# New step orders, an earlier load of q for pair 1, and five row groups stored by column halves in a fused sparse-attention and soft-MoE kernel

## The chip, the core and the metric

The kernel runs on one core of a Trainium2 chip. The core has five engines with a queue of instructions each: PE (TensorE: matmuls and, beside them, weight loads, called PEld), DVE (VectorE), ACT (ScalarE), POOL (GpSimd) and SP (SyncE, which here only issues DMAs). They share nothing but memory and semaphores: an instruction waits at the head of its queue until what it needs is done, and everything behind it on that engine waits too. Sixteen DMA engines move data between HBM and the core's memory SBUF; PE writes its results to a second memory, PSUM, which DVE and ACT empty. The metric is the time of one execution on the device in microseconds (us), lower is better. Times of before and after are medians of several executions.

## What is computed

Two stages, the second on the output of the first. Batch 4, 8 heads, 768 positions, head size 64; the MoE has 8 experts of 4 slots, model size 512, hidden size 1024.

```python
def _attn_ref(q, k, v):                       # q, k, v: 4 x 8 x 768 x 64, float32
    ...
    k_min, k_max = k_chunks.min(3), k_chunks.max(3)          # chunks of 32 keys
    ub = sum over d of maximum(q * k_min, q * k_max)         # per query and chunk
    ub = where(causal, ub, -1e9); top_chunks = the 6 chunks with the largest ub
    scores = where(chosen chunk and pos_q >= pos_k, scale * q @ k.T, -1e9)
    return softmax(scores) @ v

def _moe_ref(x, phi, w1, w2):                 # x: 3072 x 512
    logits = x @ phi                                         # 3072 x 32 slots
    d = softmax(logits, axis=0); slot_input = d.T @ x
    slot_out[e] = maximum(slot_input[e] @ w1[e], 0) @ w2[e]  # 8 experts, 4 slots each
    c = softmax(logits, axis=1)
    return c @ slot_out                                      # 3072 x 512
```

## The kernel before

**Tiles and stages.** The 32 (batch, head) pairs are worked on two heads at a time, as 16 pairs 0 to 15, four to a batch. For a pair, k and q are turned (`trk`, `trq`: transposes on PE, then copies on ACT, `evk`, `evq`), the chunks' minima and maxima are taken on DVE (`kmin`, `kmax`, `bd`, which DVE or, as `bdp`, POOL does), q is split into negative and positive parts (`qsn`, `qsp`), the bound is formed on PE (`ub`), the sixth largest is found and compared on DVE (`sel`, with a cast on POOL), the comparison is turned (`ns`, `evns`). Scores are made in six groups of blocks (`sc:0` to `sc:5`, a pair of matmuls for q.k and a pair that adds the mask, lines 334 and 344), ACT takes the exponential (`ex`, line 358), POOL masks the diagonal blocks (`mk`, line 368), PE multiplies by v (`pv`, line 382), DVE divides by the row sum (`norm`, lines 394 and 395), and the result is turned (`xt`, `evx`). The MoE's logits, its running maximum over batches and the sum into slots are done once per batch (`moe_...`).

**Order of the work.** Nothing is scheduled by the compiler: `tc.manual_schedule()` keeps each engine's instructions in the order in which the program emits them. A fixed list `HEAD` does pair 0 and prepares the next ones. Then step i = 1 to 15 runs down a string of words (lines 728 to 733), in which a word acts on a pair some steps away: `sc`, `ex`, `mk` on pair i, `pv` on i - 1, `norm`, `xt`, `evx` on i - 2, `ub`, `sel`, `ns`, `evns` on i + 1, `trk` to `qsp`, `bd`, `lv` on i + 2. The word `moe_x@n` acts only where i - n is a batch's last pair. Steps 1 to 4 take PLAIN, and then by i mod 4: 0 PLAIN, 1 LOGITS, 2 SLOTS, 3 AFTER; step 14 takes BEFORE_LAST and step 15 FINAL, whose words of its own are `pl:n` (parts of the last pv), `nl`, `xl`, `el`/`ela` (its norm, transposes, and their copies on DVE or ACT), `norm1`, `xt1`, `evx1` (those of pair 14), `lgt`, `lgl` (the last logits), `cs` (column sums of the combine weights, line 817), `pma` (the last maximum), `mz` (a memset on POOL) and `lh:n` (a load of weights).

**Loads.** All loads but two come from POOL's queue and turn float32 into bf16 on the way: `lv` v of a pair (192 KB, line 174), `lkq` k and q of two pairs (384 KB each, line 168, in odd steps), `lw` weights of an expert (1 MB, line 150, in steps 2, 4, 6, 8, 9, 10, 12, 13). The second weights of the last two experts come in eight pieces of 256 KB (`w_half`, line 160): pieces 0 and 1 in step 14, 2 and 3 in step 15, 4 to 7 after it. Pieces 0 to 3 are output columns 256 to 511, pieces 4 to 7 columns 0 to 255. At the start SP loads k and q of pair 0, and POOL k of pair 1 (line 168), then the identity `ident` (line 186), q of pair 1, and k and q of pairs 2 and 3.

**The end.** After step 15 the slots go through the experts: `experts_in` (line 928), then the output projection by column halves y = 1 and y = 0: `experts_out` (line 969), `shared_out` (line 995), and `last_expert_out` (line 1005), which reads the pieces of `w_half`. The 3072 output rows are stored as 12 groups of 256 rows (512 KB). The first BYHALF groups are made and stored by column halves, so that their first halves go out between the two halves of the projection; the others follow whole:

```python
    for m in range(BYHALF):
        out_half(m, 1, TAGS[m % 2])              # 2 matmuls, line 1040; store of 256 KB, line 1042
    for f in range(2):
        experts_out(0, f)
    for f in range(2):
        shared_out(0, f)
    last_expert_out(0)
    nc.vector.tensor_scalar_mul(so_sb[0], outs[0], zinv)
    for m in range(BYHALF):
        out_half(m, 0, TAGS[(m + BYHALF) % 2])
    for m in range(BYHALF, NM):                  # whole groups: line 1070, store of 512 KB, line 1076
        ...                                      # the last one as two stores, line 1074
        if m == BYHALF:
            last_rows()                          # combine weights of the last batch
```

A group's two halves of the rows are copied from PSUM by DVE (line 1029) and ACT (line 1026) side by side; SP issues the stores.

Of the kernel before, what the change touches and what calls it, by code (L numbers as in the profile page):

```python
# [59 lines left out]
def kernel(  # L60
# [13 lines left out]
    NPB = H // 2  # L74
# [88 lines left out]
    def load(i, nm, n=1):  # L163

        b, j = divmod(i, NPB)
        t = ring[nm][i // 2 % 3][:, 2 * (i % 2):2 * (i % 2 + n)]
        src = {"k": k, "q": q}[nm][b, 2 * j:2 * (j + n)]
        nc.gpsimd.dma_start(out=t, in_=src.rearrange("h (p g) d -> p h (g d)", p=P))
        for x in range(n):
            st[nm, i + x] = t[:, 2 * x:2 * x + 2]  # L170
# [15 lines left out]
    nc.gpsimd.affine_select(
        out=ident, in_=ident, compare_op=ALU.not_equal, fill=1.0, base=0,
        pattern=[[-1, P]], channel_multiplier=1,
# [9 lines left out]
    nc.vector.memset(pm_pad, 0.0)  # L198
    nc.vector.memset(pm_lo, 0.0)

    load(1, "q")
    load(2, "k", 2)
    load(2, "q", 2)
    def spread_mask(t0, t1, copy):
# [520 lines left out]
            }[name]  # L725
            moe(fn, i - off)

    PLAIN = """sc:0 trk lv sc:1 norm ex:0 ex:1 ub sc:2 pv:0 mk:0 evk pv:5 sel sc:5 mk:1 lw trq xt ex:2 pv:2 ex:5 evq pv:3:1 sc:3 kmin sc:4 kmax ex:3 ex:4 evx qsn ns mk:5 pv:4 mk:4 evns mk:2 mk:3 qsp lkq bd"""
    LOGITS = """sc:0 trk sc:2 ex:0 ub norm ex:2 sc:3 evk mk:0 lv pv:0 pv:5 pv:1 mk:2 sc:1 sel ex:3 xt kmin pv:2 trq pv:3 ex:1 evq sc:5 lw ex:5 mk:1 sc:4 evx ns kmax bd mk:3 moe_logits@2 evns mk:5 qsn lkq ex:4 moe_copy@2 moe_lo@2 mk:4 qsp pv:4"""
    SLOTS = """sc:1 ex:1 mk:1 moe_max@3 sc:2 ex:2 mk:2 ub moe_bound@3 norm sel moe_comb@3 trk evk sc:0 sc:3 ex:0 moe_exp@3 lkq ex:3 mk:3 pv:0:1:2:3 trq xt kmin evq moe_exp2@3 evx kmax bd moe_scale@3 lv lw sc:5 ex:5 mk:5 sc:4 ex:4 mk:4 ns evns mk:0 moe_dispatch@3 pv:5 moe_comb2@3 qsn qsp pv:4"""  # L730
    AFTER = """sc:0 lv trk sc:2 ex:0 ex:2 evk ub sc:1 norm pv:0 pv:5 sel ex:1 pv:2 pv:3 mk:0 sc:3 pv:1 mk:2 xt trq lw ex:3 sc:5 kmin evx evq ex:5 sc:4 ns mk:1 kmax bdp pv:4 mk:5 evns ex:4 mk:4 lkq qsp moe_ct@4 mk:3 qsn"""
    BEFORE_LAST = """lv norm sc:2 ex:2 moe_max@3 sc:4 ex:4 sc:0 moe_bound@3 moe_comb@3 mk:4 lw ub sel sc:3 pv:0 trk evk pv:2 moe_exp@3 pv:3:4:5:1 mk:2 ex:0 trq evq kmin sc:5 ex:3 mk:0 moe_comb2@3 kmax moe_exp2@3 xt ns sc:1 moe_scale@3 mk:3 lkq qsn ex:5 lh:0 evx mk:5 ex:1 qsp lh:1 evns moe_dispatch@3 moe_ct3@3 bd mk:1"""
    FINAL = """sc:1 sc:0 norm sc:2 ex:1 pv:0 pv:2 pv:3 pv:4 mk:1 ctc pv:5 pv:1 ex:0 ex:2 sc:3 xt mk:0 ex:3 norm1 sc:4 mk:2 ex:4 xt1 mk:3 evx pl:0 evx1 sc:5 mk:4 pl:2 pl:1 nl:0 pl:3 nl:1 xl:0 pl:4 el:0 mz lh:2 ex:5 pl:5 lh:3 lgt:0 xl:1 lgt:1 nl:2 lgl:0 xl:2 ela:1 lgl:1 el:2 lgl:2 pma cs"""

    BL = B - 1
    parts = {}
# [285 lines left out]
    def rows(m):  # L1022
        return out[m * 2 * P:(m + 1) * 2 * P, :].rearrange("(p x) d -> p x d", x=2)
# [40 lines left out]
    n = 0  # L1064
    for m in range(BYHALF, NM):
        o_sb = op.tile([P, 2, Dm], F32, name="o_sb", tag="o_sb")
# [8 lines left out]
        if m < NM - 1:  # L1075
            nc.sync.dma_start(out=rows(m), in_=o_sb)
        if m == BYHALF:
            last_rows()
# [30 lines left out]
```

## Time and profile before

| What | us |
|---|---|
| Median of 3 executions | 156.44 (156.4 to 156.86) |
| The profiled execution's own time | 156.91 |
| Its span, first to last instruction | 155.2 |
| PE busy | 137.7 |
| DVE busy | 122.4 |
| ACT busy | 122.0 |
| POOL busy | 95.6 |
| First store issued | 134.63 |
| Last store issued | 150.38 |

The profile is of one execution; its span lies inside its own time. Times in it count from the span's start. "Busy" is time in which an engine's instructions ran; a long chain of short waits can hide behind a high share. "Idle before" says how long an engine did nothing before an instruction and, behind an arrow, what ended that. The DMA share counts packets in flight over 16 engines, so it can be above 1. A DMA's "us to landing" runs from its issue to the last of its data.

### The profile page before, as it was taken

Reading aid. Unit: us, or ns where it says so; the run is one execution under the profiler, and the core shown is the slowest. Engines: PE = TensorE matmul, PEld = TensorE weight load, DVE = VectorE, ACT = ScalarE, POOL = GpSimd, SP = SyncE. Lnnn points to the kernel's source line nnn. Section 1 sums busy time; section 2 is a strip of 40 time slices with the busy share of each in tenths; the row PEclk is TensorE's granted clock in tenths of the full one; section 3 lists DMA queues with packets and bytes.
Section 4 is the critical chain, followed back from the end, with each engine's and each line's share of the span. In section 5 each row is a group of like instructions: output and inputs, shape, how many; then the busy total and the mean of one; then the engine's idle time right before and its main releaser. Section 6 shows DMA issues by size and latency. Waiting matters only on the chain.

```text
span 155.2 us, 6083 instructions
## 1 busy us (share of the span) xinstructions
PE 137.7 (89%) x2512; PEld 91.0 (59%) x2513; DVE 122.4 (79%) x450; ACT 122.0 (79%) x166; POOL 95.6 (62%) x196
## 2 busy tenths in 40 slices
PE   7989998999999989999999999999989999776700
PEld 2444565667667676766767675766767755553200
DVE  4777987999899999999999999999766642449800
ACT  3678999999999999999999999999886233527700
POOL 6966698964978669486936947496783980000000
PEclk9999999999999999999999999999999999999965
DMA  4999999999999999999999999999999999999995
GB/s 161 184 181 207 202 191 195 214 180 196 209 215 194 196 207 189 197 205 215 202 191 200 202 211 195 206 186 213 212 200 215 211 196 198 168 313 320 378 406 229
DMA packets 46171, 33.31 MB, mean 215 GB/s; under 512 B 26304, under 2 KB 41664, under 8 KB 46144
## 3 DMA queue, kind: packets, MB, share of 16 engines
q0 software_dynamic: 41328, 25.86, 115.0%
q1 hardware_dynamic: 4816, 7.08, 12.5%
q8 instruction: 19, 0.31, 0.7%
q14 instruction: 8, 0.07, 0.1%
HBM read 52.49 MB, written 6.29 MB: 379 GB/s over the span
## 4 chain that ended last, share of the span: by engine, by line
PE 43%; DVE 17%; ACT 11%; POOL 9%; DMA 9%; issue 4%; DVEq 0%; SPq 0%; ACTq 0%; POOLq 0%
PE at_ps L382 10%; PE sc_ps L334 10%; ACT e_sb L358 9%; PE sc_ps L344 7%; DMA w_half<-in_moe_w_dram 7%; PE tr_ps L225 5%; PE xT_ps L404 3%; PE ub_ps L284 2%; POOL w_half L160 2%; DMA w_sb<-in_q_dram 2%; DVE mx L305 2%; POOL e_sb L368 2%; PE ns_ps L316 2%; DVE o_sb L1029 2%; DVE mm L244 2%
## 5 line engine op out<-in xcount | busy, mean ns | idle before, releaser
L358 ACT ACTIVATE e_sb<-sc_ps 128x768 bf16<-128x768 f32 (+2 forms) x96 | 83.2, 928 | 4.7 <-PE sc_ps L344 4.3
L368 POOL TENSOR_SCALAR_AFFINE_SELECT e_sb<-e_sb 128x256 bf16<-128x256 bf16 x96 | 37.8, 413 | 17.9 <-ACT e_sb L358 17.6
L334 PE MATMUL sc_ps<-qT,kT 64*128 64x384 bf16 (+3 forms) x260 | 37.6, 306 | 0.9 <-ACT e_sb L358 0.7
L344 PE MATMUL sc_ps<-nsT,smask 64*128 64x384 bf16 (+2 forms) x296 | 37.6, 284 | 0.1
L382 PE MATMUL at_ps<-v_t,e_sb 128*128 128x65 bf16 x630 | 26.2, 193 | 0.2
L382 PEld LDWEIGHTS <-e_sb 128*128 128x128 bf16 x630 | 22.4, 97 | 5.2 <-issue 3.1
L305 DVE MAX8 mx<-ub_ps 128x8 f32<-128x8 f32 (+1 forms) x192 | 16.9, 165 | 4.7 <-PE ub_ps L294 4.0
L334 PEld LDWEIGHTS <-kT 64*128 64x128 bf16 x260 | 12.8, 93 | 8.0 <-issue 2.2
L174 POOL DMA_DIRECT2D v_t<-in_v_dram x16 | 16.7, 1045 | 1.0 <-DMA w_sb<-in_moe_w_dram 0.9
L344 PEld LDWEIGHTS <-smask 64*128 64x128 bf16 x296 | 14.9, 95 | 3.3 <-issue 0.4
L395 DVE TENSOR_TENSOR x_sb<-at_ps,inv 128x768 bf16<-128x768 f32 (+3 forms) x18 | 15.6, 869 | 0.6
L244 DVE TENSOR_REDUCE mm<-kT 128x24 bf16<-128x768 bf16 x16 | 15.1, 943 | 0.1
L250 DVE TENSOR_REDUCE mm<-kT 128x24 bf16<-128x768 bf16 x16 | 15.1, 943 | 0.0
L235 ACT COPY qT<-tr_ps 128x768 bf16<-128x768 bf16 x16 | 13.1, 816 | 1.7 <-PE tr_ps L225 1.7
L235 ACT COPY kT<-tr_ps 128x768 bf16<-128x768 bf16 (+1 forms) x16 | 12.7, 795 | 0.6 <-PE tr_ps L225 0.6
L415 DVE COPY xT_sb<-xT_ps 128x768 bf16<-128x768 bf16 (+2 forms) x17 | 8.8, 518 | 1.6 <-PE xT_ps L404 1.6
L150 POOL DMA_DIRECT2D w_sb<-in_moe_w_dram x14 | 10.1, 721 | 0.0
L215 PE MATMUL warm_ps<-ones_sq 128*128 128x512 bf16 x27 | 8.8, 449 | 1.1 <-DVE ones_sq L180 1.1
L284 PEld LDWEIGHTS <-qpn 128*128 128x128 bf16 x192 | 6.1, 96 | 5.1 <-issue 3.7
L404 PE MATMUL xT_ps<-ident,x_sb 128*128 128x128 bf16 x96 | 8.4, 220 | 0.2 <-DVE xT_sb L415 0.2
L284 PE MATMUL ub_ps<-bd,qpn 128*128 128x48 bf16 x192 | 7.8, 184 | 0.5 <-DVE bd L256 0.4
L308 DVE TENSOR_TENSOR ns_t<-ub_ps,mx 128x288 bf16<-128x288 f32 x16 | 7.3, 457 | 0.5
(171 smaller groups left out, 220.9 us busy)
## 6 DMA issues: line engine op xcount, KB each, us to landing
w_sb<-in_moe_w_dram POOLq DMA_DIRECT2D x14, 1024.0 KB, 17.6
out_dram<-o_sb SPq DMA_DIRECT2D x14, 256.0 KB, 3.8
v_t<-in_v_dram POOLq DMA_DIRECT2D x16, 192.0 KB, 13.9
out_dram<-o_sb SPq DMA_DIRECT2D x5, 512.0 KB, 4.4
w_half<-in_moe_w_dram POOLq DMA_DIRECT2D x8, 256.0 KB, 10.4
k_in<-in_k_dram POOLq DMA_DIRECT2D x5, 384.0 KB, 13.7
q_in<-in_q_dram POOLq DMA_DIRECT2D x5, 384.0 KB, 12.3
w_sb<-in_k_dram POOLq DMA_DIRECT2D x2, 384.0 KB, 11.7
```

The lines of the kernel that those rows point to most:

```text
L174: nc.gpsimd.dma_start(out=v_t[i % NV][:, :, :, :D], in_=v[b, 2 * j:2 * j + 2].rearrange("h (g p) d -> p h g d", p=P),)
L235: copy(t.rearrange("d (p g) -> d p g", g=NQT)[:, :, g0:g1], ps.rearrange("d g p -> d p g"),)
L244: nc.vector.tensor_reduce(mm[:, 0, 0, :], kT, axis=AX.X, op=ALU.min)
L250: nc.vector.tensor_reduce(mm[:, 1, 0, :], kT, axis=AX.X, op=ALU.max)
L284: nc.tensor.matmul(o, lhsT=qpn[:, x, t * P:(t + 1) * P], rhs=bd[:, x], start=(t == 0 and x == 0), stop=False,)
L305: nc.vector.max(mx[:, a, :], ub[:, a, :max(8, 4 * t + 4)])
L334: nc.tensor.matmul(ps[:, h, c:c + w], lhsT=kT[r, kg * P:(kg + 1) * P], rhs=qT[r, qs], start=True, stop=False,)
L344: nc.tensor.matmul(ps[:, h, c + (f - t0) * P:c + (l - t0) * P], lhsT=smask[r, x, kg].rearrange("p a b -> p (a b)"), rhs=nsT[r, (f - x * NJ ...
L358: nc.scalar.activation(e[:, :, :w], st.pop(("scps", i, g))[:, :, :w], func=ACT.Exp, scale=scale)
L368: nc.gpsimd.affine_select(out=e[:, :, c:c + P], in_=e[:, :, c:c + P], compare_op=ALU.is_ge, fill=0.0, base=0, pattern=[[0, 2], [1, P]], ch ...
L382: nc.tensor.matmul(o, lhsT=st["e", i, g][:, h, c:c + P], rhs=v_t[i % NV][:, h, kg, :D + 1], start=(kg == 0), stop=(kg == t),)
L395: nc.vector.tensor_tensor(st["x", b][:, t0:t1, 2 * j:2 * j + 2, :].rearrange("p t h d -> p h t d"), at[:, :, :, :D], inv.broadcast_to([P, ...
```

## The change

Three things. POOL issues the load of q of pair 1 right behind that of k of pair 1, ahead of `ident`. All step strings are new, and a new one, REST, takes PLAIN's place in steps 8 and 12; REST also does the transposes of a batch's combine weights (`moe_ct@5`) that AFTER did one step before (`moe_ct@4`). And BYHALF is 5.

```diff
--- before.py
+++ after.py
@@ -183,6 +183,7 @@
     for t, src in zip(stage, (k, q)):
         nc.sync.dma_start(out=t, in_=src[0, :2].rearrange("h (p g) d -> p h (g d)", p=P))
     load(1, "k")
+    load(1, "q")
     nc.gpsimd.affine_select(
         out=ident, in_=ident, compare_op=ALU.not_equal, fill=1.0, base=0,
         pattern=[[-1, P]], channel_multiplier=1,
@@ -198,7 +199,6 @@
     nc.vector.memset(pm_pad, 0.0)
     nc.vector.memset(pm_lo, 0.0)
 
-    load(1, "q")
     load(2, "k", 2)
     load(2, "q", 2)
     def spread_mask(t0, t1, copy):
@@ -725,12 +725,13 @@
             }[name]
             moe(fn, i - off)
 
-    PLAIN = """sc:0 trk lv sc:1 norm ex:0 ex:1 ub sc:2 pv:0 mk:0 evk pv:5 sel sc:5 mk:1 lw trq xt ex:2 pv:2 ex:5 evq pv:3:1 sc:3 kmin sc:4 kmax ex:3 ex:4 evx qsn ns mk:5 pv:4 mk:4 evns mk:2 mk:3 qsp lkq bd"""
-    LOGITS = """sc:0 trk sc:2 ex:0 ub norm ex:2 sc:3 evk mk:0 lv pv:0 pv:5 pv:1 mk:2 sc:1 sel ex:3 xt kmin pv:2 trq pv:3 ex:1 evq sc:5 lw ex:5 mk:1 sc:4 evx ns kmax bd mk:3 moe_logits@2 evns mk:5 qsn lkq ex:4 moe_copy@2 moe_lo@2 mk:4 qsp pv:4"""
-    SLOTS = """sc:1 ex:1 mk:1 moe_max@3 sc:2 ex:2 mk:2 ub moe_bound@3 norm sel moe_comb@3 trk evk sc:0 sc:3 ex:0 moe_exp@3 lkq ex:3 mk:3 pv:0:1:2:3 trq xt kmin evq moe_exp2@3 evx kmax bd moe_scale@3 lv lw sc:5 ex:5 mk:5 sc:4 ex:4 mk:4 ns evns mk:0 moe_dispatch@3 pv:5 moe_comb2@3 qsn qsp pv:4"""
-    AFTER = """sc:0 lv trk sc:2 ex:0 ex:2 evk ub sc:1 norm pv:0 pv:5 sel ex:1 pv:2 pv:3 mk:0 sc:3 pv:1 mk:2 xt trq lw ex:3 sc:5 kmin evx evq ex:5 sc:4 ns mk:1 kmax bdp pv:4 mk:5 evns ex:4 mk:4 lkq qsp moe_ct@4 mk:3 qsn"""
-    BEFORE_LAST = """lv norm sc:2 ex:2 moe_max@3 sc:4 ex:4 sc:0 moe_bound@3 moe_comb@3 mk:4 lw ub sel sc:3 pv:0 trk evk pv:2 moe_exp@3 pv:3:4:5:1 mk:2 ex:0 trq evq kmin sc:5 ex:3 mk:0 moe_comb2@3 kmax moe_exp2@3 xt ns sc:1 moe_scale@3 mk:3 lkq qsn ex:5 lh:0 evx mk:5 ex:1 qsp lh:1 evns moe_dispatch@3 moe_ct3@3 bd mk:1"""
-    FINAL = """sc:1 sc:0 norm sc:2 ex:1 pv:0 pv:2 pv:3 pv:4 mk:1 ctc pv:5 pv:1 ex:0 ex:2 sc:3 xt mk:0 ex:3 norm1 sc:4 mk:2 ex:4 xt1 mk:3 evx pl:0 evx1 sc:5 mk:4 pl:2 pl:1 nl:0 pl:3 nl:1 xl:0 pl:4 el:0 mz lh:2 ex:5 pl:5 lh:3 lgt:0 xl:1 lgt:1 nl:2 lgl:0 xl:2 ela:1 lgl:1 el:2 lgl:2 pma cs"""
+    PLAIN = """norm sc:0 trk ex:0 sc:1 ub pv:0 lv pv:5 sc:2 ex:1 sel mk:1 evk ex:2 sc:5 trq ex:5 mk:0 evq mk:5 pv:2 pv:3 pv:1 xt kmin sc:3 sc:4 ex:3 ex:4 kmax lw evx ns mk:4 qsn evns pv:4 mk:2 lkq mk:3 qsp bd"""
+    REST = """lv moe_ct@5 sc:1 norm trk ex:1 sc:2 ub sc:0 ex:2 pv:0:5 evk mk:2 ex:0 sc:3 trq sel mk:1 lkq xt lw pv:1 kmin pv:2 ex:3 mk:0 evx sc:5 sc:4 kmax pv:3 evq bdp mk:3 ex:5 ns qsn ex:4 evns mk:5 pv:4 mk:4 qsp"""
+    LOGITS = """sc:0 trk sc:2 ex:0 lv ub mk:0 norm lw sc:1 sel pv:0 ex:2 pv:1 pv:2:5 evk sc:3 xt ex:1 trq kmin ex:3 evx sc:5 evq sc:4 kmax mk:1 ns mk:2 ex:5 moe_logits@2 qsn mk:5 bd mk:3 evns ex:4 moe_copy@2 moe_lo@2 mk:4 qsp pv:3 pv:4 lkq"""
+    SLOTS = """sc:2 moe_max@3 ex:2 mk:2 sc:1 moe_comb@3 moe_bound@3 ex:1 ub norm sel trk evk sc:5 sc:0 ex:5 moe_exp@3 ex:0 pv:0 mk:1 pv:3 moe_exp2@3 pv:5:1 trq xt evq lkq kmin lv pv:2 kmax evx moe_scale@3 sc:4 lw ex:4 sc:3 mk:0 ns ex:3 mk:3 evns bdp moe_comb2@3 mk:4 qsn pv:4 mk:5 qsp moe_dispatch@3"""
+    AFTER = """sc:1 ex:1 norm sc:0 trk ub ex:0 sc:2 pv:0 pv:3:2 evk lv pv:5 sc:3 mk:0 sel ex:2 mk:2 kmin pv:1 xt trq ex:3 evx mk:1 kmax sc:5 sc:4 ns lkq evq lw ex:5 pv:4 bdp mk:3 qsp ex:4 evns qsn mk:4 mk:5"""
+    BEFORE_LAST = """norm sc:2 lv sc:4 moe_max@3 ex:2 ub moe_bound@3 ex:4 moe_comb@3 sel sc:0 pv:0:2 trk moe_exp@3 pv:3:4:5:1 evk mk:4 sc:3 kmin trq ex:0 moe_comb2@3 kmax evq qsp ex:3 bd moe_exp2@3 ns xt moe_scale@3 evx mk:2 mk:0 sc:1 evns ex:1 lh:0 lw sc:5 ex:5 mk:5 mk:3 qsn moe_dispatch@3 moe_ct3@3 lh:1 lkq mk:1"""
+    FINAL = """sc:1 norm sc:0 sc:2 ex:1 ex:0 pv:0:4 pv:2 pv:3:5:1 ex:2 mk:0 sc:3 ctc xt mk:1 mk:2 ex:3 mk:3 sc:4 ex:4 norm1 xt1 mk:4 sc:5 pl:0 evx evx1 ex:5 nl:0 pl:1 pl:3 lh:2 pl:2 pl:4 xl:0 nl:1 lh:3 ela:0 mz pl:5 lgt:0 lgt:1 lgl:0 nl:2 xl:2 cs xl:1 el:1 ela:2 lgl:1 lgl:2 pma"""
 
     BL = B - 1
     parts = {}
@@ -828,7 +829,7 @@
             for y in range(2):
                 w_half[LATE[i - E], y] = wt.tile([P, NFG, Dm // 2], BF16, name=f"w_half{i}_{y}")
         order = FINAL if i == LAST else BEFORE_LAST if i == LAST - 1 else PLAIN if i <= NPB else (
-            PLAIN, LOGITS, SLOTS, AFTER)[i % NPB]
+            REST, LOGITS, SLOTS, AFTER)[i % NPB]
         for what in order.split():
             if what.startswith("lh:"):
                 load_w_half(int(what[3:]))
@@ -1030,7 +1031,7 @@
 
     w_ctx.close()
     op = ctx.enter_context(tc.tile_pool(name="op", bufs=NM))
-    BYHALF = 6
+    BYHALF = 5
     o_tiles = [op.tile([P, 2, Dm], F32, name="o_sb", tag="o_sb") for _ in range(BYHALF)]
 
     def out_half(m, y, tags):
```

## The prediction

> **What bounds the kernel now.** I read the page first, then busy times by window, then the last 45 us in order of time, then each DMA from issue to landing.
>
> ```profile
> PE 137.7 (89%) x2512; PEld 91.0 (59%) x2513; DVE 122.4 (79%) x450; ACT 122.0 (79%) x166; POOL 95.6 (62%) x196
> DMA  4999999999999999999999999999999999999995
> GB/s 161 184 181 207 202 191 195 214 180 196 209 215 194 196 207 189 197 205 215 202 191 200 202 211 195 206 186 213 212 200 215 211 196 198 168 313 320 378 406 229
> ```
>
> PE is the busiest engine, but the DMA row reads 9 in 38 of 40 slices. The table by window (sum of the stretch, then PE, PEld, DVE, ACT, POOL, clock, DMA share, GB/s) says the same:
>
> ```profile
> 27.64:33.99 6.35, 6.35 (x128) 4.37 (x126) 5.98 (x25) 6.34 (x10) 5.63 (x12) 1.00 1.39 198
> 25.00:118.00 93.00, 91.24 (x1831) 64.00 (x1827) 85.92 (x320) 88.28 (x115) 68.02 (x144) 1.00 1.38 201
> 140.00:142.00 2.00, 1.70 (x11) 0.87 (x10) 1.94 (x5) 1.89 (x6) 0.00 (x0) 1.00 0.83 288
> 142.00:144.00 2.00, 1.02 (x14) 0.68 (x14) 1.43 (x4) 0.67 (x2) 0.00 (x0) 1.00 1.04 350
> 146.00:148.00 2.00, 0.32 (x2) 0.00 (x0) 1.65 (x3) 1.04 (x2) 0.00 (x0) 1.00 1.02 408
> ```
>
> Over 93 us of the steps the DMA engines' share is 1.38 (packets in flight, over 1 means always something queued). Do compute or loads end last? The chain of waits near its end, and two DMA rows (the last 1 MB of w_sb, issued at 104.65, and the last w_half, issued at 127.65; KB, us to landing):
>
> ```profile
> 127.65 10.47 DMA w_half<-in_moe_w_dram
> 138.16 0.32 PE so_last L1005 x4
> 138.50 0.50 DVE so_all L1060
> ```
> ```profile
> w_sb<-in_moe_w_dram POOLq DMA_DIRECT2D x1, 1024.0 KB, 22.7
> ```
>
> w_sb lands at 104.65 + 22.7 = 127.35 and the last of the eight 256 KB pieces of w_half at 127.65 + 10.47 = 138.12. So the eight landed one behind the other, 10.77 / 8 = 1.35 us each, and a load waits 10 to 23 us in the queue behind others. That is a stream of loads that never runs dry: it ends when its bytes are through, whenever they were issued. PE in order of time (start, duration, line, idle before it):
>
> ```profile
> 132.53 0.57 PE L1005 MATMUL so_ps<-w_half,hT_pad 128*32 128x256 bf16 x8
> 133.67 0.60 PE L1040 MATMUL oh_ps<-so_all,cT_all 128*128 128x256 bf16 x4 [0.57 <-ACT so_all L1051]
> 136.06 1.06 PE L969 MATMUL so_last<-w_sb,hT_pad 128*32 128x256 bf16 x32
> 137.59 0.28 PE L1005 MATMUL so_last<-w_half,hT_pad 128*32 128x256 bf16 x4
> 138.16 0.29 PE L1005 MATMUL so_last<-w_half,hT_pad 128*32 128x256 bf16 x4 [0.28 <-DMA w_half<-in_moe_w_dram]
> ```
>
> PE came to the last four matmuls 0.28 us before their weights. The first eight (at 132.53) are as tight: the fourth piece landed at 127.35 + 4 x 1.35 = 132.75, and the second four of that row began near 132.8. Both halves of the output projection start when weights land; compute is level with them, not behind.
>
> After that come the stores. SP's issues (start, duration) and, under each, its KB and us to landing:
>
> ```profile
> 139.97 0.53 SPq L1042 DMA_DIRECT2D out_dram<-o_sb  x1
> 143.29 0.56 SPq L1042 DMA_DIRECT2D out_dram<-o_sb  x1
> 143.96 0.58 SPq L1076 DMA_DIRECT2D out_dram<-o_sb  x1
> 147.91 1.15 SPq L1076 DMA_DIRECT2D out_dram<-o_sb  x1
> 150.38 1.15 SPq L1074 DMA_DIRECT2D out_dram<-o_sb  x1
> ```
> ```profile
> out_dram<-o_sb SPq DMA_DIRECT2D x1, 256.0 KB, 2.9
> out_dram<-o_sb SPq DMA_DIRECT2D x1, 256.0 KB, 3.0
> out_dram<-o_sb SPq DMA_DIRECT2D x1, 512.0 KB, 3.6
> out_dram<-o_sb SPq DMA_DIRECT2D x1, 512.0 KB, 4.9
> out_dram<-o_sb SPq DMA_DIRECT2D x1, 256.0 KB, 3.7
> ```
>
> The second wave of halves lands from 139.97 + 2.9 = 142.87 to 143.29 + 3.0 = 146.29: (146.29 - 142.87) / 5 = **0.68 us a half**. Whole groups land from 147.56 to 152.81 in four steps: **1.31 us each**. The last store lands at 154.08, with computing over at 147.65. Only between 140 and 142 do the engines have slack (share 0.83): the first six halves are through and the next ones have just begun.
>
> **The change part by part.**
>
> *BYHALF 6 to 5.* The sixth group leaves both waves and becomes a whole store behind them. From the start of the second wave, 5 halves and 7 whole groups have to land instead of 6 and 6: +1.31 - 0.68 = **+0.63 us**. Its half in the first wave filled the slack before the second wave, so leaving it out frees nothing. What could pay: PE comes to L1005 earlier by one group. Six groups took DVE this long:
>
> ```profile
> 133.98 2.70 DVE L1029 TENSOR_SCALAR o_sb<-oh_ps,inv_a 128x256 f32<-128x256 f32 x6 [1.99 <-DMA w_half<-in_moe_w_dram]
> ```
>
> 2.70 / 6 = 0.45 us. But PE was already 0.28 us early; it will wait 0.28 + 0.45 = 0.73 us for the same w_half instead. Gain 0 if the stream ends at 138.12, at most 0.73. last_rows moves up one group and feeds the same full queue: 0.
>
> The whole store also saves one issue. Two half spacings are 1.36 us and one whole group 1.31, so that is worth 0.05, already in the sum. The Trainium skill, "DMA: Bandwidth & Descriptors", section "Anatomy of one DMA — SWDGE (gpsimd) path", gives each DMA about 2.0 us fixed and the rest by bytes; taken as serial costs, one DMA fewer would give -2.0 instead of -0.05, which spacings of 0.68 contradict here.
>
> *Loads.* By the diff the three kinds (lv, lw, lkq) keep their order within the odd and even steps that use them, so the stream carries the same bytes in the same order. Later issues (lv of the plain step now stands behind pv:0) are covered by 10 to 23 us of queue. Value 0. What moves its end is other traffic:
>
> ```profile
> q8 instruction: 19, 0.31, 0.7%
> ```
>
> 19 fetches of 16 KB in 0.7% of 16 x 155.2 us are 0.9 us of one engine each. A fetch that falls on the engine that is last adds up to that; one more or fewer there is **-0.9 to +0.9**, and I take 0. (The Trainium skill, "Runtime: NRT & Kernel Launch", "Instruction fetch mechanics", calls crossing a 16 KiB block "mostly hidden"; by that the term would be 0 on both sides, and the row, which shows time on the engines that carry the weights, keeps the range.) The three runs, 156.4 to 156.86, spread by half of it.
>
> *q of pair 1 sooner.* POOL's queue and its readers:
>
> ```profile
> 2.25 0.30 POOL L186 TENSOR_SCALAR_AFFINE_SELECT ident<-ident 128x128 bf16<-128x128 bf16 x1
> 2.49 0.73 POOL L168 DMA_DIRECT2D q_in<-in_q_dram  x1
> 4.30 1.00 PE L225 MATMUL tr_ps<-ident,k_in 128*64 128x128 bf16 x12
> 10.36 0.53 PE L225 MATMUL tr_ps<-ident,q_in 128*64 128x128 bf16 x12
> q_in<-in_q_dram POOLq DMA_DIRECT2D x1, 192.0 KB, 6.1
> ```
>
> q moves up by 0.3 us; it landed at 8.59 and was read at 10.36 with no wait: gain 0. ident is done 0.73 us later, near 3.3, and first read at 4.30: cost 0; if that cover were gone, 0.7. Every later instruction of POOL stays.
>
> *The orders.* Counts of exp, score, mask and pv work stay. In PLAIN sc:2 moves next to sc:5, so PE changes between score and pv work once less:
>
> ```profile
> 27.06 0.34 PE L334 MATMUL sc_ps<-qT,kT 64*128 64x384 bf16 x2
> 27.23 0.33 PE L344 MATMUL sc_ps<-nsT,smask 64*128 64x384 bf16 x2
> 27.49 0.60 PE L382 MATMUL at_ps<-v_t,e_sb 128*128 128x65 bf16 x14
> ```
>
> Two pairs started 0.17 apart, so 27.40 is where a third would have started; pv came at 27.49: 0.09 us, four PLAIN steps, -0.4. For REST, LOGITS, SLOTS, AFTER and BEFORE_LAST the trace holds no such order. The gain is bounded by ACT's idle time, 93.00 - 88.28 = 4.7 us; the loss by a wait such as ACT's 1.07 us below, in each of 15 steps, 16 us. SLOTS hands bd (0.25 us) from DVE to POOL; REST takes moe_ct from AFTER. I take -0.5 in all, nearer to the row of PLAIN. In FINAL:
>
> ```profile
> 117.84 2.01 ACT L358 ACTIVATE e_sb<-sc_ps 128x1024 bf16<-128x1024 f32 x2 [1.07 <-PE sc_ps L344]
> 122.82 0.59 PE L817 MATMUL h_ps<-live,cT_all 128*128 128x1 bf16 x18
> 123.02 0.36 DVE L803 TENSOR_REDUCE pm<-lgt_ps 128x32 f32<-128x192 f32 x1 [0.30 <-PE lgt_ps L427]
> ```
>
> The column sums (0.59 us) ran beside pma; now they stand ahead of xl:1 and so on the path to pma: +0.6. el:0 (0.35 us) leaves DVE's path for ACT: about -0.35. Net +0.2. Compute in all: about 0.3 us sooner, and none of it arrives: PE waits longer at L1005, twice.
>
> **Sum.** +0.63 + 0 + 0 + 0 = about +0.6 us. On the profiled execution (156.91 with a span of 155.2) that is 157.5 and 155.8; the median is 0.47 lower, so 156.44 + 0.6 = **157.0**.
>
> **The rivals.**
>
> *Compute becomes late.* Decides when the new orders cost over 0.73 us by L1005; then the end moves one for one. For it: ACT and PE are idle 0.01 us and less in a PLAIN step, so any new wait counts. Against: 0.73 of slack. With 1.5 to 2 us lost: 157.8 to 158.3.
>
> *The stream ends sooner (not slower).* If the last w_half lands 0.6 us or more earlier, by a fetch that misses the last engine (0.9), the second wave starts up to 0.73 earlier: 156.44 + 0.63 - 0.73 = 156.3, and no lower unless compute gains too. Against: same bytes, same order.
>
> *The orders' gain arrives.* It needs the loads to follow compute, POOL's issues being the limit. Then -0.5 to -4.7 counts: say 155.2. Against: 10 to 23 us of waiting loads.
>
> *A store fewer is a fixed cost less.* A store alone takes 2.9 us and lands 0.68 behind another: 2.2 us fixed. Were these serial, 156.44 + 0.63 - 2.2 = 154.9. Against: they overlap in every row above. (The page on DMA named above is read this way.)
>
> **How the numbers follow.** Forecast 0.50 (156.5 to 157.5); compute late 0.22; stream sooner 0.17; orders arrive 0.09; fixed cost 0.02. A measurement tells about 0.3% (0.47 us) from no change. Of the forecast's 0.50, 0.10 lies within that; of the stream's 0.17, 0.16; of the orders' 0.09, 0.01. Same 0.27; faster 0.01 + 0.08 + 0.02 = 0.11; slower 0.40 + 0.22 = 0.62. Range: 156.44 + 0.63 - 0.9 = 156.1 below, a fetch less; 158.1 above, 1 us of late compute and some. That leaves out about 0.19.
>
> **What would show it.** Right: the last w_half lands near 138.1; PE waits about 0.7 us on it at L1005; the second wave starts near 140.0; DMA share below 0.8 just before; last store near 154.7. Wrong: w_half well before 137.5, or a PE that comes to L1005 after its weights.

## The result and the profile after

| | before | after |
|---|---|---|
| Median of 7 executions, us | 156.65 | 157.55 |
| Lowest to highest, us | 156.28 to 157.94 | 157.1 to 158.77 |
| The profiled execution's own time, us | 156.91 | 157.15 |

The ratio of after to before is 1.0059, with a 95% interval of 1.0034 to 1.0084: about 0.9 us slower, 0.5 to 1.3. The prediction was 157.0, from 156.1 to 158.1.

The page of after has the same shape as that of before: a DMA row of nines but for one 8, and one new mark in the row of the granted clock, a 5 in the 33rd slice.

```profile
PE 137.3 (88%) x2510; PEld 91.0 (59%) x2511; DVE 120.2 (77%) x444; ACT 121.3 (78%) x166; POOL 97.4 (63%) x200
PEclk9999999999999999999999999999999959999955
DMA  4999999999999999999999999999999999998995
GB/s 148 213 182 209 201 194 194 216 177 194 216 212 195 192 211 187 196 211 211 197 195 205 198 212 197 201 191 216 204 205 213 209 199 194 150 299 305 395 404 227
```

The chain that ended last in after has the same link between loads and stores as before. Columns are start, duration, what.

```profile
127.35 10.48 DMA w_half<-in_moe_w_dram
...
137.88 0.32 PE so_last L1006 x4
...
138.22 0.49 DVE so_all L1061
```

The last piece of w_half landed at 127.35 + 10.48 = 137.83 (138.12 before). PE's rows around it in after, then ACT's copies of k in three PLAIN steps (1, 2 and 3) and its first exponentials of the last step:

```profile
125.64 3.70 PE L929 MATMUL h_ps<-w_sb,siT_pad 128*32 128x512 bf16 x48
132.84 0.39 PE L1006 MATMUL so_ps<-w_half,hT_pad 128*32 128x256 bf16 x8
137.48 0.69 PE L1006 MATMUL so_last<-w_half,hT_pad 128*32 128x256 bf16 x8
21.01 0.79 ACT L235 COPY kT<-tr_ps 128x768 bf16<-128x768 bf16 x1
27.28 0.79 ACT L235 COPY kT<-tr_ps 128x768 bf16<-128x768 bf16 x1
33.63 0.82 ACT L235 COPY kT<-tr_ps 128x768 bf16<-128x768 bf16 x1
113.12 2.43 ACT L358 ACTIVATE e_sb<-sc_ps 128x1024 bf16<-128x1024 f32 x3 [0.20 <-PE sc_ps L344]
```

The rows of before that answer to the first and to the last four of these:

```profile
126.25 2.77 PE L928 MATMUL h_ps<-w_sb,siT_pad 128*32 128x512 bf16 x48 [0.16 <-DVE siT_pad L904]
20.89 0.79 ACT L235 COPY kT<-tr_ps 128x768 bf16<-128x768 bf16 x1
27.64 0.79 ACT L235 COPY kT<-tr_ps 128x768 bf16<-128x768 bf16 x1
33.99 0.82 ACT L235 COPY kT<-tr_ps 128x768 bf16<-128x768 bf16 x1
114.34 2.43 ACT L358 ACTIVATE e_sb<-sc_ps 128x1024 bf16<-128x1024 f32 x3 [0.56 <-PE sc_ps L344]
```

Follow the lead of after over before down these rows. At the same group of exponentials (the 91st of 96 and the next two) after is 114.34 - 113.12 = **1.22 us ahead**. When the slots go through the experts it is 126.25 - 125.64 = **0.61 ahead**. These 48 matmuls then take 3.70 us and not 2.77, so 0.93 is lost; at the first L1006 after is 132.84 - 132.53 = **0.31 behind**. A lead of more than twice the prediction's 0.5 came up in the steps, and it was gone before the output. One pair of profiles is little for that, but all of them agree: from the first exponential to the 91st, the six profiles with the old step orders (before and, below, e1, e3, e5, s1, s2) took 101.70 to 102.29 us, the eight with the new ones 100.45 to 100.86.

What the stores did, in after: the first store of the second wave and the last store of all, and under them their KB and us to landing.

```profile
139.67 0.54 SPq L1043 DMA_DIRECT2D out_dram<-o_sb  x1
150.54 1.18 SPq L1075 DMA_DIRECT2D out_dram<-o_sb  x1
```
```profile
out_dram<-o_sb SPq DMA_DIRECT2D x1, 256.0 KB, 2.4
out_dram<-o_sb SPq DMA_DIRECT2D x1, 256.0 KB, 3.8
```

The last store landed at 154.29 (150.54 and 3.75; the row rounds). From 139.67 on the stores took 154.29 - 139.67 = **14.62 us**, where before took 154.08 - 139.97 = **14.11**. The second wave starts 0.30 sooner and lasts 0.51 longer. The windows of after (sum, PE, PEld, DVE, ACT, POOL, clock, DMA share, GB/s) show where:

```profile
140.00:142.00 2.00, 1.65 (x12) 0.90 (x11) 1.79 (x4) 1.90 (x5) 0.00 (x0) 1.00 0.77 267
142.00:144.00 2.00, 1.25 (x10) 0.66 (x12) 1.34 (x4) 0.73 (x2) 0.00 (x0) 1.00 1.00 344
146.00:148.00 2.00, 0.20 (x1) 0.00 (x0) 1.53 (x3) 0.85 (x2) 0.00 (x0) 1.00 1.00 401
```

From 142 the queue is as full as before (shares 1.00, before 1.04 and 1.02), but the slack at the start of the second wave has grown: share 0.77 for 0.83.

And the 5 in the clock's row: two stretches of after, one behind the other, and the stretch of before with the same work as the first.

```profile
120.74:124.15 3.41, 2.72 (x40) 1.59 (x39) 1.57 (x7) 0.49 (x2) 3.41 (x5) 1.00 1.11 212
124.15:127.57 3.42, 3.42 (x48) 1.64 (x49) 1.53 (x8) 0.97 (x3) 1.98 (x4) 0.50 1.35 195
```
```profile
121.53:124.95 3.42, 3.15 (x50) 2.04 (x48) 2.03 (x9) 0.65 (x2) 3.42 (x6) 1.00 1.12 208
```

In after the granted clock is 0.50 for 3.42 us, while PE is busy throughout; in the 3.41 us ahead PE had been busy 2.72. In before it was busy 3.15 in that place and the clock stayed.

### The profile page after: what moved, and what is told of

Its sections match the earlier page's. It is cut to its first block, busy times and chain, and to the rows that moved or that the text cites. A ratio compares the mean times of both kernels' runs of the same rounds, so it can differ in the third digit from the quotient of the medians.

```text
span 155.4 us, 6099 instructions
## 1 busy us (share of the span) xinstructions
PE 137.3 (88%) x2510; PEld 91.0 (59%) x2511; DVE 120.2 (77%) x444; ACT 121.3 (78%) x166; POOL 97.4 (63%) x200
## 4 chain that ended last, share of the span: by engine, by line
PE 60%; DMA 9%; DVE 9%; POOL 8%; issue 4%; ACT 4%; DVEq 0%; SPq 0%; POOLq 0%; ACTq 0%
PE sc_ps L334 13%; PE at_ps L382 13%; PE sc_ps L344 10%; DMA w_half<-in_moe_w_dram 7%; PE tr_ps L225 7%; PE xT_ps L404 4%; PE ub_ps L284 3%; ACT e_sb L358 3%; PE ns_ps L316 3%; DMA w_sb<-in_q_dram 2%; DVE o_sb L1030 2%; POOL w_half L160 1%; POOL e_sb L368 1%; POOL v_t L174 1%; PE lg_ps L427 1%
## 5 line engine op out<-in xcount | busy, mean ns | idle before, releaser
L358 ACT ACTIVATE e_sb<-sc_ps 128x1024 bf16<-128x1024 f32 (+2 forms) x96 | 83.2, 931 | 4.5 <-PE sc_ps L344 4.3
L334 PEld LDWEIGHTS <-kT 64*128 64x128 bf16 x260 | 13.5, 93 | 8.4 <-issue 1.8
L415 DVE COPY xT_sb<-xT_ps 128x768 bf16<-128x768 bf16 (+1 forms) x16 | 8.6, 534 | 1.9 <-PE xT_ps L404 1.9
```

The source lines that it names most:

```text
L334: nc.tensor.matmul(ps[:, h, c:c + w], lhsT=kT[r, kg * P:(kg + 1) * P], rhs=qT[r, qs], start=True, stop=False,)
L358: nc.scalar.activation(e[:, :, :w], st.pop(("scps", i, g))[:, :, :w], func=ACT.Exp, scale=scale)
```

## The experiments

Two theories. **A**, that of the prediction: the stream of loads sets when the output can be made and the queue of stores ends last; BYHALF at 5 costs about 0.6 us by itself, and the orders and q give nothing that arrives. **B**, the rival that after's trace suggests: BYHALF costs little, and the new orders cost, through the clock that falls at 124.

### The parts alone

e1 is before with one edit, e2 is after with one edit, and e3 is before with the load of q moved:

```diff
--- e1_five_only, against before
-    BYHALF = 6
+    BYHALF = 5
--- e2_six_back, against after
-    BYHALF = 5
+    BYHALF = 6
--- e3_q_only, against before
     load(1, "k")
+    load(1, "q")
...
-    load(1, "q")
     load(2, "k", 2)
```

> The kernel before with BYHALF 5 and nothing else. Load theory (the end is set by the landing of the last w_half and by the queue of stores behind it): five halves and seven whole groups land behind the second wave's start instead of six and six, 1.31 - 0.68 = +0.6 us (between +0.4 and +0.8), and PE waits about 0.7 us for the last w_half instead of 0.28. Order theory (the loss of the change comes from its new step orders, and PE's 0.45 us gained by a group fewer in the first wave pays for the later store): 0, between -0.2 and +0.2.

> The changed kernel with BYHALF back at 6: the new orders and the earlier q alone. Load theory: the orders' gain before the tail (ACT's last exponentials began 1.2 us sooner in the profile after) is absorbed by the wait for the last w_half; 0, between -0.3 and +0.3 against the kernel before. Order theory: most of the measured +0.9 us stays, +0.5 to +0.9.

> The kernel before with only the load of q of pair 1 issued ahead of the identity. Load theory: 0, between -0.2 and +0.2; the first exponential starts about 0.1 us later, as in the profile after (12.41 for 12.29), and nothing of that is left at the end. Rival (the queue of POOL at the start matters): the end moves with the head, +0.1 to +0.3.

| | ratio to before | 95% interval |
|---|---|---|
| e1_five_only | 1.0038 | 1.0009 to 1.0067 |
| e2_six_back (orders and q) | 1.0008 | 0.9981 to 1.0034 |
| e3_q_only | 1.0000 | 0.9973 to 1.0026 |

BYHALF alone is +0.6 us (0.1 to 1.0), and the orders with q are +0.1 with bounds of -0.3 and +0.5; B falls. Together 1.0046, within the interval of after. In e1 PE comes to the last weights early and waits, as forecast:

```profile
137.65 0.29 PE L1005 MATMUL so_last<-w_half,hT_pad 128*32 128x256 bf16 x4 [0.61 <-DMA w_half<-in_moe_w_dram]
```

In this profiled execution the last piece landed at 137.61, 0.5 sooner than in that of before, and the stores from 139.45 to 154.09 took 14.64 us: so its end was that of before (154.08). That is one execution, 156.96, and 0.3 below e1's median. The length of the stores is steady from run to run; where the stream ends is not.

### The length of the stores, by BYHALF

e4 is after with BYHALF at 7, e5 is before with it.

> The changed kernel with BYHALF 7. Load theory: one more group fills the store queue's slack before the second wave; against the changed kernel two whole stores behind the wave become halves, up to -1.3 us, less what PE's later arrival at the last weights costs (two groups more in the first wave are 0.9 us, of which 0.7 us and more was waiting); -0.3 to -1.0 us against the changed kernel, that is -0.1 to +0.6 against the kernel before. Order theory: two groups more are 0.9 us of DVE and ACT in the first wave and move the end later: +0.5 us against the changed kernel.

> The kernel before with BYHALF 7. Load theory: one whole store behind the second wave becomes a half in front of it (-0.63 us), at most the 0.35 us for which the DMA engines stood idle between 140.5 and 141.5, and PE comes 0.45 - 0.28 = 0.17 us late to the last weights: between -0.4 and +0.1 us. Order theory: 0.45 us more of first wave, +0.2 to +0.5. If PE's wait ahead of the second half grows so that the granted clock falls there, as it did with the clock held at 124 (0.5 from 135.2 to 138.6): +0.3 to +0.9.

e4 came to 1.0003 (0.998 to 1.0025), e5 to 0.9989 (0.9965 to 1.0013). From the first store of the second wave to the last landing, in all profiles but those of h2 and h3, which come below:

| BYHALF | kernel | from | to | us |
|---|---|---|---|---|
| 5 | after | 139.67 | 154.29 | 14.62 |
| 5 | e1 | 139.45 | 154.09 | 14.64 |
| 6 | before | 139.97 | 154.08 | 14.11 |
| 6 | e2 | 139.97 | 154.08 | 14.11 |
| 6 | e3 | 139.32 | 153.43 | 14.11 |
| 6 | s1, s2, s3, f1 (below) | 141.73, 139.58, 138.66, 140.55 | 155.86, 153.68, 152.75, 154.64 | 14.13, 14.10, 14.09, 14.09 |
| 7 | e4 | 140.22 | 153.81 | 13.59 |
| 7 | h1 (below) | 141.03 | 154.62 | 13.59 |
| 7 | e5 | 140.51 | 154.29 | 13.78 |

A group moved out of the halves costs 0.52 us here (the prediction had 0.63). But a group more also lies on PE's way to the second wave. From the first matmul of the first wave to the first of the next projection (lines 1040 and 969 of before), PE takes 2.13 us with five groups, 2.39 with six and 3.07 with seven, in every one of these profiles in which the clock holds there. So the sixth group puts 0.26 us in front of the second wave (the prediction had 0.45), and the seventh 0.68. e4's second wave starts 0.25 later than e2's, e5's 0.54 later than before's; a part of the 0.54 is a stream of loads that ended 0.38 later in e5's execution (138.50). In e5 that takes the whole saving back (its end is 154.29, that of before 154.08), in e4 half of it, and seven is no gain that can be measured. Five is the one that costs, because what PE saves there then only lengthens its wait for the weights.

The same profiles show that the loads hold more than PE. In all twelve that keep the last expert's pieces, the first store of the first wave lands 0.66 to 0.73 us after the last w_half, though it was issued 2.8 to 4.6 us ahead of that landing; by then 0.4 to 1.0 of the 6.3 MB of output have moved. From the last w_half to the last store it is 15.95 to 15.97 us with six halves (before, e2, e3), 16.46 and 16.48 with five (after, e1), and with seven 15.79 in e5 and 16.31 in e4, where PE reached its last weights 0.94 us after they landed. Twelve groups at 1.31 us are an estimated 15.7. So with six halves the store queue hardly runs dry behind the last load, seven have about 0.2 to gain, and five leave a hole between the waves (DMA share 0.54 from 140 to 141 in after, 0.76 in before).

### Is it the stream of loads?

s1 is before with one more load of 256 KB put ahead of the eight pieces of w_half. s2 is before without the four loads of the last expert's pieces; its matmuls read the pieces of the expert before instead, so it leaves out the last expert's second weights. s3 is after with BYHALF at 6, the same loads left out, and two pairs of matmuls that do nothing put into FINAL (`kp`, behind `xl:1` and behind `lgl:2`).

```diff
--- s1_one_more_load, against before
...
+            nc.gpsimd.dma_start(
+                out=spare_w, in_=moe_w2[0].rearrange("(a p x) d -> a p x d", p=P, x=4)[0, :, :, :Dm // 2])
--- s2_before_less, against before (in s3 too)
+        if e == LATE[-1]:
+            return
...
-                rhs=w_half[LATE[-1], y][:, fg, :],
+                rhs=w_half[LATE[-2], y][:, fg, :],
--- s3_after_less, against after, besides
+        if name == "kp":
+            keep(2)
...
-    BYHALF = 5
+    BYHALF = 6
```

> The kernel before with one more load of 256 KB in POOL's queue at the end of step 13, into a tile that nothing reads (its data is part of the second weights; the output is that of the kernel before). Load theory: every later load lands 1.34 us later, so both halves of the projection start later by that much, and the end moves by +1.3 us (+1.1 to +1.5). Order theory (compute sets the end, loads are hidden): 0 to +0.2.

> The kernel before without the four w_half pieces of the last expert; its output projection reads the pieces of the expert before instead, so that part of the output is left wrong in value while all instructions but the four loads stay. The stream of loads ends 5.4 us sooner. Load theory: compute, which in the kernel before came to its weights 0.28 us early, now sets the end: about -0.3 us (-0.6 to 0). Order theory: 0.

> The changed kernel with BYHALF 6, without the same four pieces (the same part of the output is left wrong), and with two pairs of filler matmuls in the last step, so that PE's granted clock does not fall to 0.5 for 3.4 us as it did at 124.2 in the profile after (the window of 3.4 us before that fall had PE busy 2.72 us; the same stretch of the kernel before had 3.15). Load theory: with the loads out of the way the 1.2 us that the new orders gain before the tail reach the end: -1.0 to -1.6 us against the kernel before, 0.7 to 1.3 below the kernel before with the same loads left out. Order theory (the orders lose): +0.3 to +0.9.

s1: 1.0088 (1.006 to 1.0116), +1.4 us for one piece of 1.35 us. s2: 0.9966 (0.995 to 0.9983), -0.5. s3: 0.9927 (0.9906 to 0.9947), -1.1. So one load more costs about its own length (0.9 to 1.8 by the interval), and four less (5.4 us of stream) give before only 0.5: its compute stands right behind. With the same loads gone, the new orders and the held clock are worth another 0.6 us. The first stores of the second wave, of s2 and of s3:

```profile
139.58 0.53 SPq L1044 DMA_DIRECT2D out_dram<-o_sb  x1
```
```profile
138.66 0.53 SPq L1047 DMA_DIRECT2D out_dram<-o_sb  x1
```

That is 0.92 us in the traces, and s3's end is 0.93 sooner; its experts start 0.92 sooner too (125.57 and 126.49). So with the loads gone the lead that is left at the experts arrives whole, and what keeps it from the output of after is the stream in part and the clock in part.

s1 also shows what such a wait sets off. PE's row at the four matmuls that lacked their weights, and then two windows of s1:

```profile
133.52 0.29 PE L1008 MATMUL so_ps<-w_half,hT_pad 128*32 128x256 bf16 x4 [1.01 <-DMA w_half<-in_moe_w_dram]
```
```profile
132.69:136.10 3.41, 1.67 (x12) 0.97 (x12) 1.41 (x4) 1.73 (x5) 0.00 (x0) 1.00 1.30 178
136.08:139.49 3.41, 3.28 (x52) 2.15 (x55) 1.24 (x3) 1.34 (x4) 0.00 (x0) 0.50 1.10 294
```

The wait of 1.01 us leaves PE busy 1.67 of 3.41, the clock falls to 0.50 right behind it, and PE reaches its last weights at 139.82, 0.98 us after they landed (138.84). In this profiled execution the stream ended only 0.72 later than in before (its last w_sb had come at 126.77, 0.59 sooner than that of before), so here the clock and not the last piece set the second wave: the 1.4 us of s1 are in part the load's own and in part what the wait for it set off. Its four executions fit that, though they are few: the two with the higher mean clock (0.984 and 0.980) took 157.71 and 157.62, the others (0.966, which is the profiled one, and 0.976) 158.70 and 158.58.

### Which part of the orders loses the lead?

f1 is after with BYHALF at 6 and the FINAL of before (its old line in the diff above); all other orders are the new ones.

> The changed kernel with BYHALF 6 and the string FINAL of the kernel before; all other new orders stay. If the new FINAL (column sums ahead of the last transposes) makes the stretch of little PE work, the clock does not fall at 124 and the experts start 0.9 us or more ahead of those of the kernel before (126.25). Load theory for the end: 0, between -0.3 and +0.3 against the kernel before, since PE then waits the longer for the weights. Order theory: the gain of the other orders arrives, -0.5 to -1.2.

f1: 1.0035 (1.0009 to 1.0061); the expected end was that of before, so this missed. Its rows of PE and two of its windows:

```profile
125.03 2.77 PE L929 MATMUL h_ps<-w_sb,siT_pad 128*32 128x512 bf16 x48 [0.16 <-DVE siT_pad L905]
132.34 0.29 PE L1006 MATMUL so_ps<-w_half,hT_pad 128*32 128x256 bf16 x4 [0.76 <-DMA w_half<-in_moe_w_dram]
138.63 0.39 PE L1006 MATMUL so_last<-w_half,hT_pad 128*32 128x256 bf16 x8
```
```profile
131.47:134.88 3.41, 1.78 (x17) 0.97 (x12) 1.37 (x4) 1.68 (x5) 0.00 (x0) 1.00 1.30 178
134.88:138.29 3.41, 3.26 (x48) 2.10 (x51) 1.27 (x3) 1.36 (x4) 0.00 (x0) 0.50 1.04 279
```

The first row answers the question: with the old FINAL the experts start at 125.03, 126.25 - 125.03 = 1.22 ahead of before, the whole lead, at full clock. So the new FINAL costs 125.64 - 125.03 = 0.61 us here and brings the fall at 124 (e2 and e4, with the new FINAL, have it too). Most of the 0.61 is lost ahead of that fall, by the last maximum (`pma`). DVE's rows there, of after and then of f1:

```profile
122.33 0.36 DVE L804 TENSOR_REDUCE pm<-lgt_ps 128x32 f32<-128x192 f32 x1 [0.36 <-PE lgt_ps L427]
```
```profile
121.79 0.36 DVE L804 TENSOR_REDUCE pm<-lgt_ps 128x32 f32<-128x192 f32 x1 [0.30 <-PE lgt_ps L427]
```

That is 0.54. In all profiles the way from the 91st exponential to the experts is 11.91 or 11.92 us with the old FINAL, 12.52 to 12.88 with the new one and the fall (after, e4, e2), and 12.39 to 12.43 where added matmuls hold the clock (s3 and the h kernels below).

But keeping the lead made f1 slower, not faster: PE now waits 0.76 us for the fourth piece (landed 132.30), PE is busy 1.78 of 3.41, the clock falls at 134.88, and PE reaches the last weights at 138.63, 0.63 after they landed. Its second wave starts at 140.55. Earlier compute, in front of a stream that had hardly moved (its last piece landed at 138.00, that of before at 138.12), ended later here.

### Can the lead be kept?

The three h kernels are after with BYHALF at 7 and the two `kp` of s3, which hold the clock at 124. h2 adds eleven matmuls of 256 columns that do nothing to the first wave, h3 three of 512 columns; h3 also has three `kp` matmuls instead of four, and three of the warming matmuls (`w:1`) at the start are left out.

```diff
--- h2_seven_filled, against after, besides kp and BYHALF = 7 (h1 has only these)
+    def fill(n):
+        for _ in range(n):
+            nc.tensor.matmul(so_last, lhsT=ident, rhs=w_sb[E][:, :HD], start=True, stop=True)
+    fill(4)
...
+        fill(1)
--- h3_seven_lean, against h2
-            nc.tensor.matmul(so_last, lhsT=ident, rhs=w_sb[E][:, :HD], start=True, stop=True)
+        nc.tensor.matmul(so_two[:, 1, :], lhsT=ident, rhs=w_sb[E][:, :512], start=True, stop=True)
...
-    fill(4)
+    fill()
...
-        fill(1)
+        if m in (1, 3):
+            fill()
```

> The changed kernel with BYHALF 7 and the two pairs of filler matmuls in the last step, output as the reference. If a stretch with little PE work is what drops the clock, the granted clock stays at 1.00 from 5 to 145 us, the first 48 matmuls of the experts take 2.8 us instead of 3.7, and PE comes to the last w_half 0.5 to 0.9 us sooner than with BYHALF 7 alone (138.33 there, with the weights landed at 137.5): -0.3 to -0.6 us against that kernel and against the kernel before. If the clock's fall has another cause: still 3.4 us at 0.5, and the time of BYHALF 7 alone, 0 against the kernel before.

> The changed kernel with BYHALF 7, the two pairs of filler matmuls in the last step and, new, filler matmuls in the first wave (four ahead of it, one behind each group), output as the reference. If the fall of the clock at 135.2 in the run before came of PE's waits between 131.8 and 135.2 (busy 2.08 us of 3.4), the clock now holds to 140, PE comes to the last w_half near 138.0 instead of 139.1 and the second wave starts near 139.9 instead of 141.0: -0.7 to -1.1 us against that run, -0.2 to -0.6 against the kernel before. If the clock falls all the same, or for another reason: 0 to +0.4 against the kernel before.

> The kernel after with seven of the eight row groups by halves, two filler pairs in the last step, only three filler matmuls of 512 columns in the first wave (eleven of 256 before), and three of the warming matmuls at the start left out, so that the program has fewer PE instructions than the one in which a twentieth instruction fetch fell among the stores. If that fetch was what cost h2_seven_filled its gain: no fetch between 140 and 152, the clock at 1.0 to 145, PE at the last expert weights at 137.7 to 138.0, the second wave's first store at 139.7 to 139.9, the end at 153.1 to 153.5, the time 0.6 to 1.1 us below the kernel before and 1.1 to 1.6 us below h2. If the fetch was a bystander and the stores are late for another reason: 0.3 to 1.0 us above the kernel before, as h2. If three fillers don't hold the clock: it falls at 135, the second wave's first store comes near 141 and the time is about 0.3 us above the kernel before, as h1.

h1: 1.0029 (1.001 to 1.0049). h2: 1.0068 (1.004 to 1.0097). h3: 1.0023 (1.0009 to 1.0037). All three missed their favoured case. h1 went the way of f1; its two windows:

```profile
131.80:135.20 3.40, 2.07 (x26) 1.17 (x15) 1.65 (x4) 1.96 (x5) 0.00 (x0) 1.00 1.26 172
135.21:138.62 3.41, 3.27 (x46) 1.96 (x48) 1.46 (x4) 1.55 (x4) 0.00 (x0) 0.50 1.01 281
```

In h2 the clock held through the output and the second wave started at 139.65, as expected, but the stores took 15.26 us where seven halves took 13.59 to 13.78. First the issues of two stores (SP), then each one's KB and us to landing, then the DMA queues between 143.7 and 146.8, and two windows:

```profile
140.96 0.57 SPq L1045 DMA_DIRECT2D out_dram<-o_sb  x1
141.63 0.63 SPq L1045 DMA_DIRECT2D out_dram<-o_sb  x1
```
```profile
out_dram<-o_sb SPq DMA_DIRECT2D x1, 256.0 KB, 3.4
out_dram<-o_sb SPq DMA_DIRECT2D x1, 256.0 KB, 5.1
```
```profile
q8 instruction: 1, 0.02, 2.9%
```
```profile
145.00:146.00 1.00, 0.89 (x4) 0.13 (x2) 1.00 (x3) 1.00 (x3) 0.00 (x0) 1.00 0.82 282
146.00:147.00 1.00, 0.00 (x0) 0.00 (x0) 1.00 (x2) 0.61 (x2) 0.00 (x0) 1.00 0.74 253
```

One store lands at 140.96 + 3.35 = 144.31, the next at 146.71, 2.4 us later and not 0.68. Between them stands an instruction fetch, the twentieth of this program, begun at 143.79: 2.9% of 16 engines for 3.1 us is 1.4 us of one engine. The shares of 0.82 and 0.74 behind it would fit a queue in which some engines have run dry while one is late. h3, with fewer PE instructions, has no fetch there (its twentieth begins at 156.12, after the last landing), its windows stay full, and its stores take 154.66 - 140.65 = 14.01 us:

```profile
145.00:146.00 1.00, 1.00 (x6) 0.45 (x5) 0.74 (x2) 0.81 (x2) 0.00 (x0) 1.00 1.04 343
146.00:147.00 1.00, 0.89 (x4) 0.13 (x2) 1.00 (x3) 1.00 (x3) 0.00 (x0) 1.00 1.00 349
```

That speaks for the fetch, with one profile of each. The fetch is not all of h2's 15.26, though: its second wave starts 0.57 sooner than e4's, but its first wave lands no sooner (until 142.27; e4's until 142.29), and so the first half of the second wave lands at 142.96, where e4's does at 142.97. Its earlier start met a queue that was still full, and h2 ends 154.91 - 153.81 = 1.10 later than e4.

h3's stream ended late (PE's rows):

```profile
132.38 0.29 PE L1009 MATMUL so_ps<-w_half,hT_pad 128*32 128x256 bf16 x4 [0.67 <-DMA w_half<-in_moe_w_dram]
138.86 0.29 PE L1009 MATMUL so_last<-w_half,hT_pad 128*32 128x256 bf16 x4 [0.71 <-DMA w_half<-in_moe_w_dram]
```

PE was early for both sets of weights. The sixth piece had come 2.74 us after the fifth, with a fetch at 134.29 and the first stores from 134.21 in that gap, and the last one at 138.81, 1.0 later than in after. None of these kernels beats before. Why the sixth piece was so late is open: fetches at 134.3 to 134.8 stand in e1, f1, h1 and h2 too, where a piece came 0.8, 0.5, 0.6 and 0.6 us over the usual 1.34 behind the one before, which the next piece gave back in part. In the seven profiles whose fetch began at 135.1 or later no such gap is over 1.45. The records don't say which DMA engine a fetch used.

## Why the prediction was right

**The bound.** Right, with an addition. One load more of 1.35 us costs 1.4 (s1), though part of that goes by way of the clock, which the prediction did not have; and e1, f1 and h3 show PE waiting for w_half as soon as it comes sooner. What the prediction did not see is that the first wave's stores, too, land only behind the last w_half (0.7 us). "Compute is level with them" was right too: without the stream's last 5.4 us before gained 0.5.

**BYHALF.** Right in sign and size: +0.63 forecast, +0.6 alone (e1), 1.0059 against 1.0008 with the new orders (after against e2), and 0.51 in the traces. The prediction summed spacings, and the rows give 0.12 less: in after the first half of the second wave lands 2.45 us after its issue and not 2.93, and the halves behind it follow each other at 0.77 us and not 0.69. The forecast that PE waits 0.73 us for the last w_half came out as 0.61 in e1 and about 0.12 in after (the second four matmuls began at 137.88, and 0.28 after 137.48 would have been 137.76): there PE was only 0.11 ahead of before at these weights (137.48 against 137.59), and they came 0.29 sooner. The saving of 0.45 that went into the 0.73 was itself too large, 0.26 by PE's rows. The rival of a fixed cost for each store, -2.2 us, fell with e1. The section of the Trainium skill that the prediction names beside it, in "DMA: Bandwidth & Descriptors", is about DMAs issued from POOL's queue; these stores are issued by SP.

**Loads and fetches.** The last piece came 0.29 us sooner in after, 0.5 in e1, and 0.7 later in h3: the term of 0 with 0.9 on both sides holds these. That fetches make these differences was not shown; e3 and e5, with the loads of before, ended theirs at 137.47 and 138.50. That a fetch can also fall among the stores, as in h2, the prediction did not have.

**q.** Right, 1.0000.

**The orders.** That nothing arrives was right (1.0008). Its working was not. The lead in the steps was 1.22 us, not 0.5. The row of PLAIN that gave 0.09 a step was a wrong reading: a PLAIN step takes 33.63 - 27.28 = 6.35 us in after and 33.99 - 27.64 = 6.35 in before, and ACT is busy 6.34 of them in both, so a switch less on PE is nothing there. But step 1, which runs down the same string, takes 27.28 - 21.01 = 6.27 and 27.64 - 20.89 = 6.75: 0.48 gained, part of it in a wait of PE for POOL's `ns_t` (0.21 us, in before 0.50). Another 0.53 came in step 14, BEFORE_LAST (from its first exponential to that of step 15, 7.10 us before and 6.57 after); the steps between gave 0.33, and after had begun its first exponential 0.12 behind. FINAL was put at +0.2 and is +0.61, of which 0.54 by the last maximum. That the column sums (0.59) count whole and the copy handed from DVE to ACT gives nothing would fit this, but neither was tried alone. And the clock's 0.93 us had no term. Two misses, 0.72 of gain and 0.41 + 0.93 of loss, sit in one sum: compute was forecast 0.3 sooner and came 0.31 later. The forecast's reason, that the loads cover such a difference, held; that the misses came out at 0.31, within the slack, is luck. "PE waits longer at L1005, twice" was therefore wrong for after; f1 waited there once (0.76) and h3 twice (0.67 and 0.71).

**Signs.** Forecast: w_half near 138.1 (137.83), second wave near 140.0 (139.67), last store near 154.7 (154.29), and a DMA share below 0.8 just before the second wave (1.00 from 139 to 140, and 0.77 from 140 to 142, after its first issue and ahead of its first landing at 142.12). The whole came 0.3 to 0.4 sooner in this execution, which is 157.15 where the median is 157.55.

## What to carry to other kernels

Ask of each saving what it waits for next: here 1.22 us of faster steps met a stream of loads that had not moved, and nothing arrived until four loads were taken out. Where stores are issued behind loads that are still under way, look when the first of them lands: here that was 0.7 us after the last load, and from there the bytes of the output set the end. When stores end last, price the split between small and whole stores by their spacing in the queue, and count the work that fills the queue's first slack as well. A wait for weights that leaves PE half idle may cost again as a slower clock behind it, so getting to a fixed landing sooner can end later.

## What the runs showed of the hardware

- The granted clock fell to 0.50 for 3.41 to 3.42 us behind stretches of about the same length in which PE was busy 2.72 (after), 2.07 (h1), 1.78 (f1) and 1.67 us (s1). In the fall of after, the 48 matmuls of the experts took 3.70 us and not 2.77. The Trainium skill, "TensorE: Matmul & The Clock Gate", section "HAM oscillation — how this bites in real kernels", has it fall when PE stands idle longer than a window of about 3.4 us. The length of the fall agrees with that window; the condition does not: PE stood idle for 0.7 to 1.7 us of such a stretch, all its gaps together.
- Busy time alone does not decide it either. In e2 the stretch below has PE busy 2.22 us, less than the 2.72 of after, and the granted clock stays at 1.00 in it and behind it. The stretch of after is full of small matmuls (1, 32 and 64 columns). Whether that decides was not tried; two pairs of 480 columns put into it held the clock there (s3, h1, h2), and so did three such matmuls in h3.

```profile
144.10:147.50 3.40, 2.22 (x8) 0.64 (x7) 3.24 (x5) 2.95 (x5) 0.00 (x0) 1.00 1.02 383
```

- A fetch of 16 KB of instructions took 1.4 us in h2 and stands in a gap of 2.4 us between two stores where 0.68 is usual; h3, without a fetch there, has no such gap. The Trainium skill, "Runtime: NRT & Kernel Launch", section "Instruction fetch mechanics", calls such a crossing "mostly hidden"; if the fetch made the gap, which one profile of each suggests, it was not hidden where the stores end last.
- The first store, issued 2.8 to 4.6 us ahead of the last load's landing, landed 0.66 to 0.73 us behind it in the twelve profiles with all loads. Without the last four loads it landed 2.5 us after its own issue (s2, s3).
